# Moving transposes of a routed-attention kernel from TensorE to DMA, and re-timing its weight loads

## The chip, the cores and the metric

The kernel runs on one core of one Trainium2 chip. A core has five engines that run side by side and wait for each other through semaphores: TensorE (PE: matmuls; PEld is its weight load), VectorE (DVE), ScalarE (ACT), GpSimd (POOL) and SyncE (SP), which here only issues DMAs. The metric is the device time of one execution in microseconds (us). A profile shows one execution; its span is about 1.8 us shorter than that execution's time, because it starts with the first instruction and ends with the last. The granted clock is the share of TensorE's full clock that the execution had. A run counts as slow when it is over 1.5% above the fastest of the same kernel, and otherwise as fast; unless said otherwise all runs compared are fast ones.

## The reference

```python
# q, k, v: (4, 8, 768, 64)   centroids: (8, 16, 64)   w_in: (512, 2048)   w_out: (2048, 512)
q_assign = argmax(q_n @ c_n.T)            # each query and key gets one of 16 clusters
k_assign = argmax(k_n @ c_n.T)
scores = where(q_assign[:, None] == k_assign[None, :], q @ k.T / sqrt(64), -1e9)
attn = softmax(scores) @ v                # per batch and head: 32 "heads" in the kernel
x = attn, heads side by side              # (3072, 512)
out = gelu(x @ w_in) @ w_out              # erf form of gelu
```

## The kernel before

The kernel goes through 32 heads (4 batches of 8). Each head has six slots, one for each 128 keys. A slot does two score matmuls on PE into one of two PSUM buffers (`ps_sc`), and ACT takes their exponential. In the same slots PE does the attention-value matmuls (AV) of the head before. After the 8 heads of a batch come 16 groups of the up projection (`fc1`); the down projection (`fc2`) is spread over the slots of the next heads.

Before its slots, a head has to be prepared: POOL splits q and k into two fp16 halves (`split`), they are transposed (`T`), PE multiplies them with the centroids (`asn`), DVE makes one-hot assignments (`onehot`), and these are transposed too and put as 16 more rows into `T`, so that the score matmul adds the mask. For heads up to 11 PE does both transposes and DVE copies them out of PSUM; from head 12 on DMA transposes on the SP queue do it. The attention output of a pair of heads is transposed as well (`fin`), by PE and a DVE copy for pairs 0 to 6, by DMA from pair 8 on, but for the last pair. ("Pair 4" is heads 4 and 5.)

```python
t_pool = ctx.enter_context(tc.tile_pool(name="tT", bufs=9))
ps_sc = ctx.enter_context(tc.tile_pool(name="ps_sc", bufs=2, space=PSUM))   # scores, fc1
ps_a = ctx.enter_context(tc.tile_pool(name="ps_a", bufs=1, space=PSUM))     # assignments: one buffer
ps_o = ctx.enter_context(tc.tile_pool(name="ps_o", bufs=2, space=PSUM))     # transposes, fc2
# ... cut ...
w_chunks = [(w_in_sb[:, m], w_in_r[:, m]) for m in range(NM)]                # 8 chunks, 512 KB each
w_chunks += [(w_out_sb[:, 4 * f:4 * f + 4], w_out_r[:, 4 * f:4 * f + 4])
             for f in range(4)]
# ... cut ...
    def tr_pe(i, w, copy=None, pool=None):
        if i not in Ts:
            Ts[i] = t_pool.tile([128, 2, S], FP16, tag="T", name="T")
        st = sts[i]
        pl, tag = pool or (ps_o, "op")
        t_ps = pl.tile([128, S], FP16, tag=tag, name="tr_ps")
        for j in range(N):
            nc.tensor.transpose(t_ps[:, j * 128:(j + 1) * 128], st[:, w, j, :], ident)
        (copy or nc.vector.tensor_copy)(Ts[i][:, w, :], t_ps)
    # ... cut ...
    def tr(i):
        st = sts.pop(i)
        Ts[i] = t_pool.tile([128, 2, S], FP16, tag="T", name="T")
        nc.sync.dma_start_transpose(
            out=Ts[i].rearrange("c w (n p) -> c (w n) p", p=128),
            in_=st.rearrange("p w n c -> p (w n c)"))
    # ... cut: asn(i, which): 6 matmuls of T with the centroids, into ps_a;
    #     onehot(i): DVE adds the halves (asum), takes the maximum, compares ...
    def ohtr(i):
        oh = ohs[(i // 2) % NOH]
        ohTs[i] = t_pool.tile([128, N, 128], FP16, tag="ohT", name="ohT")
        nc.sync.dma_start_transpose(out=ohTs[i],
                                    in_=oh.rearrange("p n a b c -> p (n a b c)"))
        ohTs[i] = ohTs[i].rearrange("c n p -> c (n p)")

    def one_pe(i):
        oh = ohs[(i // 2) % NOH]
        e = i % 2
        t_ps = ps_o.tile([128, S], FP16, tag="op", name="oh_ps")
        for j in range(N):
            nc.tensor.transpose(t_ps[0:64, j * 128:(j + 1) * 128],
                                oh[:, j, e].rearrange("p b c -> p (b c)"), ident)
        nc.vector.tensor_scalar(Ts[i][D:D + C, 1, :], t_ps[32:32 + C, :],
                                -1.0, None, op0=ALU.add)
        nc.vector.tensor_scalar(Ts[i][D:D + C, 0, :], t_ps[0:C, :],
                                float(VAL), None, op0=ALU.mult)
    # ... cut: aug(i): four DVE copies from the DMA-transposed one-hots into T ...

    def scores(i, c):
        if c == 0:
            ps[i] = p_pool.tile([128, N, S], FP16, tag="p", name="p_sb")
        s_ps = ps_sc.tile([128, 2, 512], FP32, tag="sc", name="sc_ps")
        for t in range(2):
            nc.tensor.matmul(s_ps[:, t, 0:QB], Ts[i][0:D + C, 1, c * 128:(c + 1) * 128],
                             Ts[i][0:D + C, 0, t * QB:(t + 1) * QB],
                             start=True, stop=True)
        nc.scalar.activation(ps[i][:, c, :].rearrange("p (t q) -> p t q", t=2),
                             s_ps[:, :, 0:QB], ACT_FN.Exp, bias=0.0,
                             scale=float(scale))
    # ... cut ...
    def fin(i, pe=False):
        b, h = divmod(i, H)
        m = h // 2
        if m == 0:
            xts[b] = x_pool.tile([128, NM, S], FP16, tag="xt", name="xt")
        xt, x_tok = xts[b][:, m, :], xtoks.pop(i)
        if pe:
            t_ps = ps_o.tile([128, S], FP16, tag="op", name="fin_ps")
            for j in range(N):
                nc.tensor.transpose(t_ps[:, j * 128:(j + 1) * 128],
                                    x_tok[:, j].rearrange("p a d -> p (a d)"), ident)
            nc.vector.tensor_copy(xt, t_ps)
        else:
            nc.sync.dma_start_transpose(
                out=xt.rearrange("c (n p) -> c n p", p=128),
                in_=x_tok.rearrange("p n a d -> p (n a d)"))
    # ... cut ...
    def slot(i, c):
        if i < NH:
            scores(i, c)
        if i in WARM:
            warm(WARM[i])
        fill(FILL.get((i, c), 2))
        if i >= 1:
            for j in (AVS0 if i < 10 else AVS).get(c, ()):
                av(i - 1, j)
            if c == 5:
                norm(i - 1)

    def load_w(n):
        nc.gpsimd.dma_start(out=w_chunks[n][0], in_=w_chunks[n][1])
    # ... cut: every call is an event with a nominal time; they are emitted in that order,
    #     and each engine runs its own instructions in the order of emission ...
    PT = 12
    FC1 = {(9, 3): 0, (18, 0): 1, (26, 0): 2}
    # ... cut ...
            if (i, c) in FC1:
                b = FC1[i, c]
                at(t, fill, 1000)
                for f in range(NF):
                    at(t + f * 1.3, fc1, b, f)
                    if b == 0 and f % 4 == 0:
                        at(t + f * 1.3, load_w, 4 + f // 4)
                t += NF * 1.3
                at(t - 0.01, start_fc2, b)
            TS[i, c] = t
            if c == 0:
                T.append(t)
            at(t, slot, i, c)
    # ... cut ...
    for m in range(NM):
        at(T[m + 2] + 1.0, load_w, m)
    sp_t = -3.7
    for h in range(4, NH):
        pair = h - h % 2
        want = T[h - 2] - 9.0 if h < PT else T[pair] - 33.0 + 4.0 * (h % 2)
        sp_t = max(sp_t + 4.2, want)
        at(sp_t, split, h, vnow=False)
        at(sp_t + 0.02, vcast, h - 3)
        at(sp_t + 0.03, load, h + 2)
        if h >= PT:
            at(max(T[pair] - 25.0 + 2.5 * (h % 2), sp_t + 3.5), tr, h)
    for h in range(NH - 3, NH):
        at(sp_t + 0.04, vcast, h)
    for h in range(1, NH):
        pair = h - h % 2
        if h == 1:
            at(g(0, 0), tr_pe, 1, 0)
            at(g(0, 0), tr_pe, 1, 1)
            at(g(0, 2), prep_asn, h)
            at(g(0, 4), one_pe, h)
        elif h < PT:
            o = 2 if h == 2 else 0
            at(g(h - 2, 0 + o), tr_pe, h, 0)
            at(g(h - 2, 2 + o // 2), tr_pe, h, 1)
            at(g(h - 2, 4 + o // 2), prep_asn, h)
            at(g(h - 1, 1 + o // 2) if h < 11 else g(10, 4), one_pe, h)
        else:
            t0 = T[pair] - 16.5 + 2.5 * (h % 2)
            at(t0, asn, h, 0)
            at(t0 + 1.2, asn, h, 1)
            at(t0 + 1.21, onehot, h)
            if h % 2 == 1:
                at(T[pair] - 12.0, ohtr, pair)
                at(T[pair] - 5.0, aug, pair)
    for h in range(0, NH - 2, 2):
        if h < 8:
            at(g(h + 3, 3) if h < 6 else g(9, 2), fin, h, pe=True)
        else:
            at(T[h + 3] + 0.1, fin, h)
```

The softmax here doesn't subtract the row's maximum and nothing guards it: scores larger than these inputs give would overflow.

## Time and profile before

| | before |
|---|---|
| time, median of 4 fast runs (lowest to highest) | 312.58 us (312.53 to 312.83) |
| span of the profile, granted clock | 310.7 us, 1.00 |
| PE busy | 302.0 us, 97% |
| first up projection starts | 58.86 us |
| heads 2 to 8, two heads together | 9.73 us |

From the page of before: part 1 (busy time, share of the span, number of instructions), the engines of the chain that ended last (part 4), and two of the DMA issues (part 6; the last figure is the median time to landing).

```profile
PE 302.0 (97%) x3118; PEld 189.1 (61%) x3118; DVE 124.3 (40%) x289; ACT 214.7 (69%) x269; POOL 107.2 (34%) x184
...
PE 92%; DVE 5%; DMA 1%; issue 1%; ACT 0%; DVEq 0%
...
T<-st SPq DMA_TRANSPOSE x20, 4.1
xt<-x_tok SPq DMA_TRANSPOSE x11, 3.8
```

PE looks like the only limit. But shares are averages. In heads 3 to 9 the view in order of time shows ACT nearly full too (start, duration, engine, line, operation, output and input, count; idle time before it and what ended it):

```profile
30.21 9.41 ACT L297 ACTIVATE p_sb<-sc_ps 128x768 f16<-128x768 f32 x12 [0.32 <-PE sc_ps L294]
39.94 9.41 ACT L297 ACTIVATE p_sb<-sc_ps 128x768 f16<-128x768 f32 x12 [0.32 <-PE sc_ps L294]
49.66 8.56 ACT L297 ACTIVATE p_sb<-sc_ps 128x768 f16<-128x768 f32 x11 [0.31 <-PE sc_ps L294]
58.24 1.28 ACT L354 ACT_TABLE_LOAD   x1
```

Twelve exponentials are two heads. The only gap that this view shows is one of 0.32 us every two heads, in the slot in which PE does the output transposes. The same view of PE in before, at the places where the change works:

```profile
58.52 0.51 PE L332 MATMUL fin_ps<-ident,x_tok 128*128 128x128 f16 x6 [0.61 <-DVE T L260]
58.86 20.96 PE L349 MATMUL hp<-xt,w_in_sb 128*128 128x384 f16 x128
...
85.55 0.30 PE L210 MATMUL asn_ps<-c_all,T 128*128 128x32 f16 x6 [0.59 <-DVE rec L319]
...
90.30 0.52 PE L256 MATMUL oh_ps<-ident,oh_162 128*64 128x128 f16 x6
```

PE waits 0.61 us for DVE before the output transposes that stand just ahead of the first up projection (line 349), and 0.59 us behind crowded assignments after it, where it also still transposes the one-hots of head 11. The queue of SP in before shows what a head transpose can cost when weight chunks are in flight beside it (three chunks were issued between 48.9 and 54.6 us):

```profile
49.46 13.88 SPq L192 DMA_TRANSPOSE T<-st  x2
```

### The profile page before, as it was taken

Reading aid. Unit: us, or ns where it says so; the run is one execution under the profiler, and the core shown is the slowest. Engines: PE = TensorE matmul, PEld = TensorE weight load, DVE = VectorE, ACT = ScalarE, POOL = GpSimd, SP = SyncE. Lnnn points to the kernel's source line nnn. Section 1 sums busy time; section 2 is a strip of 40 time slices with the busy share of each in tenths; the row PEclk is TensorE's granted clock in tenths of the full one; section 3 lists DMA queues with packets and bytes.
Section 4 is the critical chain, followed back from the end, with each engine's and each line's share of the span. In section 5 each row is a group of like instructions: output and inputs, shape, how many; then the busy total and the mean of one; then the engine's idle time right before and its main releaser. Section 6 shows DMA issues by size and latency. Waiting matters only on the chain.

```text
span 310.7 us, 7419 instructions
## 1 busy us (share of the span) xinstructions
PE 302.0 (97%) x3118; PEld 189.1 (61%) x3118; DVE 124.3 (40%) x289; ACT 214.7 (69%) x269; POOL 107.2 (34%) x184
## 2 busy tenths in 40 slices
PE   7999999999999999999999999999999999999995
PEld 3567777666566666656566666656566655565444
DVE  5688989500356552213155552213155413100111
ACT  3689999866768888865688788865688884466000
POOL 4999999805205204444525203454000000000000
PEclk9999999999999999999999999999999999999999
DMA  7849999998049924986668824965175302000121
GB/s 221 292 154 228 213 300 217 82 161 213 2 88 250 174 54 115 190 227 95 186 131 229 169 64 134 218 207 99 29 140 71 97 34 61 36 0 2 42 94 68
DMA packets 68449, 41.87 MB, mean 135 GB/s; under 512 B 50368, under 2 KB 64960, under 8 KB 68416
## 3 DMA queue, kind: packets, MB, share of 16 engines
q1 hardware_dynamic: 65440, 37.04, 50.4%
q0 software_dynamic: 2688, 4.19, 9.3%
q8 instruction: 24, 0.39, 0.6%
q10 hardware_dynamic: 288, 0.16, 0.2%
q14 instruction: 9, 0.07, 0.1%
HBM read 27.30 MB, written 6.29 MB: 108 GB/s over the span
## 4 chain that ended last, share of the span: by engine, by line
PE 92%; DVE 5%; DMA 1%; issue 1%; ACT 0%; DVEq 0%
PE hp L349 25%; PE op L371 24%; PE sc_ps L294 20%; PE x_ps L309 12%; PE asn_ps L210 3%; PE op_alt L371 3%; PE tr_ps L149 2%; PE oh_ps L256 1%; DVE asum L223 1%; DVE asn_ps L230 1%; DMA q_raw<-in_q_dram 1%; PE fin_ps L332 1%; PE w_ps L96 1%; DVE x_tok L320 0%; DVE T L260 0%
## 5 line engine op out<-in xcount | busy, mean ns | idle before, releaser
L297 ACT ACTIVATE p_sb<-sc_ps 128x768 f16<-128x768 f32 x192 | 150.3, 809 | 25.6 <-PE sc_ps L294 16.5
L294 PE MATMUL sc_ps<-T 80*128 80x384 f16 x384 | 93.8, 325 | 0.9 <-DVE T L280 0.4
L349 PE MATMUL hp<-xt,w_in_sb 128*128 128x384 f16 x512 | 85.7, 326 | 0.0
L309 PEld LDWEIGHTS <-p_sb 128*128 128x128 f16 x1152 | 56.4, 97 | 31.7 <-issue 0.6
L349 PEld LDWEIGHTS <-w_in_sb 128*128 128x128 f16 x512 | 48.9, 97 | 31.4
L127 POOL CAST st<-q_raw 128x384 f16<-128x384 f32 x31 | 15.8, 508 | 95.4 <-DMA q_raw<-in_q_dram 95.4
L223 DVE TENSOR_REDUCE asum<-asn_ps 128x192 f32<-128x384 f32 x31 | 17.3, 558 | 65.2 <-PE asn_ps L210 65.2
L375 DVE COPY o_sb<-op 128x512 f32<-128x512 f32 (+1 forms) x22 | 14.9, 678 | 55.9 <-PE op L371 55.8
L294 PEld LDWEIGHTS <-T 80*128 80x128 f16 x384 | 26.1, 97 | 5.9 <-ACT T L284 0.5
L128 POOL TENSOR_TENSOR st<-q_raw,st 128x384 f16<-128x384 f32 x31 | 28.3, 912 | 2.5
L130 POOL TENSOR_TENSOR st<-k_raw,st 128x384 f16<-128x384 f32 x31 | 28.3, 912 | 2.5
L319 DVE RECIPROCAL rec<-x_ps 128x6 f32<-128x6 f32 x32 | 6.2, 193 | 36.1 <-PE x_ps L309 36.0
L210 PEld LDWEIGHTS <-T 128*128 128x128 f16 x372 | 14.8, 96 | 6.8 <-issue 3.0
L210 PE MATMUL asn_ps<-c_all,T 128*128 128x32 f16 x372 | 17.3, 177 | 1.5 <-DVE rec L319 0.6
L320 DVE TENSOR_TENSOR x_tok<-x_ps,rec 128x384 f16<-128x384 f32 x32 | 17.8, 558 | 1.1
L129 POOL CAST st<-k_raw 128x384 f16<-128x384 f32 x31 | 15.5, 501 | 1.0 <-DMA k_raw<-in_k_dram 1.0
L150 DVE COPY T<-tr_ps 128x768 f16<-128x768 f16 x23 | 12.5, 552 | 1.4 <-PE tr_ps L149 1.1
L149 PE MATMUL tr_ps<-ident,st 128*128 128x128 f16 x144 | 12.1, 223 | 0.1
L230 DVE TENSOR_REDUCE asn_ps<-asum 128x12 f32<-128x192 f32 x31 | 11.2, 361 | 1.1
L149 PEld LDWEIGHTS <-st 128*128 128x128 f16 x144 | 9.4, 99 | 3.1 <-DVE st L158 1.0
L266 DVE TENSOR_SCALAR T<-ohT 16x768 f16<-16x768 f16 x20 | 7.0, 351 | 6.2 <-DMA ohT<-oh_161 2.9
L96 PE MATMUL w_ps<-wz 128*128 128x512 f16 x20 | 7.7, 470 | 1.5 <-DVE wz L78 1.5
(297 smaller groups left out, 397.6 us busy)
## 6 DMA issues: line engine op xcount, KB each, us to landing
q_raw<-in_q_dram SPq DMA_DIRECT2D x32, 192.0 KB, 3.9
k_raw<-in_k_dram SPq DMA_DIRECT2D x32, 192.0 KB, 4.0
v_raw<-in_v_dram SPq DMA_DIRECT2D x32, 192.0 KB, 4.0
out_dram<-o_sb SPq DMA_DIRECT2D x23, 256.0 KB, 2.3
w_in_sb<-in_moe_w_in_dram POOLq DMA_DIRECT2D x4, 512.0 KB, 7.4
w_out_sb<-in_moe_w_out_dram POOLq DMA_DIRECT2D x4, 512.0 KB, 11.9
T<-st SPq DMA_TRANSPOSE x20, 4.1
xt<-x_tok SPq DMA_TRANSPOSE x11, 3.8
```

The source lines that it names most:

```text
L127: nc.gpsimd.tensor_copy(st[:, 0, :, 0:D], q_raw)
L128: nc.gpsimd.tensor_sub(st[:, 0, :, D:2 * D], q_raw, st[:, 0, :, 0:D])
L130: keng.tensor_sub(st[:, 1, :, D:2 * D], k_raw, st[:, 1, :, 0:D])
L149: nc.tensor.transpose(t_ps[:, j * 128:(j + 1) * 128], st[:, w, j, :], ident)
L210: nc.tensor.matmul(a_ps[:, j, which], t[:, js], c_all[:, :, chs], start=True, stop=True)
L223: nc.vector.tensor_reduce(out=asum, in_=a_ps.rearrange("p n w l c -> p n w c l"), axis=AX.X, op=ALU.add)
L294: nc.tensor.matmul(s_ps[:, t, 0:QB], Ts[i][0:D + C, 1, c * 128:(c + 1) * 128], Ts[i][0:D + C, 0, t * QB:(t + 1) * QB], start=True, stop=True)
L297: nc.scalar.activation(ps[i][:, c, :].rearrange("p (t q) -> p t q", t=2), s_ps[:, :, 0:QB], ACT_FN.Exp, bias=0.0, scale=float(scale))
L309: nc.tensor.matmul(x_ps[:, j], ps[i][:, ch, j * 128:(j + 1) * 128], va[:, ch, :], start=(ch == 0), stop=(ch == N - 1))
L320: nc.vector.tensor_tensor(xtoks[i - i % 2][:, :, i % 2, :], x_ps[:, :, 0:D], rec.to_broadcast([128, N, D]), op=ALU.mult)
L349: nc.tensor.matmul(hp[:, t, 0:QB], w_in_sb[:, m, f * 128:(f + 1) * 128], xts[b][:, m, t * QB:(t + 1) * QB], start=(m == 0), stop=(m == NM ...
L371: nc.tensor.matmul(op[:, 0:w], gs[b][f][:, js], w_out_sb[:, f, ms], start=(f == 0), stop=(f == NF - 1))
```

## The change

Its intent: take transposes from PE where PE and DVE are full (heads 10 and 11, output pairs 0 to 2, that is `fin` of heads 0, 2 and 4) and give them to DMA; and load the weight chunks at other times, so that the DMA is free for the new transposes. Two of the chunks are held back: DVE writes one column of the chunk's destination first, so the load has to wait for DVE to come to that point.

```diff
--- before.py
+++ after.py
@@ -423,11 +423,15 @@
     def load_w(n):
         nc.gpsimd.dma_start(out=w_chunks[n][0], in_=w_chunks[n][1])
 
+    def hold_w(n):
+        nc.vector.memset(w_out_sb[:, 4 * (n - NM), 0:1], 0.0)
+
     def start_fc2(b):
         filler[0] = fc2(b)
 
 
-    PT = 12
+    PT = 10
+    WOUT_F = (2, 8, )
     FC1 = {(9, 3): 0, (18, 0): 1, (26, 0): 2}
     events = []
 
@@ -443,8 +447,10 @@
                 at(t, fill, 1000)
                 for f in range(NF):
                     at(t + f * 1.3, fc1, b, f)
-                    if b == 0 and f % 4 == 0:
-                        at(t + f * 1.3, load_w, 4 + f // 4)
+                    if b == 0 and f in WOUT_F:
+                        n = NM + 4 - len(WOUT_F) + WOUT_F.index(f)
+                        at(t + f * 1.3, hold_w, n)
+                        at(t + f * 1.3 + 0.01, load_w, n)
                 t += NF * 1.3
                 at(t - 0.01, start_fc2, b)
             TS[i, c] = t
@@ -470,7 +476,9 @@
         onehot(h)
 
     for m in range(NM):
-        at(T[m + 2] + 1.0, load_w, m)
+        at(T[m] + 6.0, load_w, m)
+    for n, w_t in enumerate((T[6] + 1.0, T[8] + 1.0, )):
+        at(w_t, load_w, NM + n)
     sp_t = -3.7
     for h in range(4, NH):
         pair = h - h % 2
@@ -497,16 +505,21 @@
             at(g(h - 2, 4 + o // 2), prep_asn, h)
             at(g(h - 1, 1 + o // 2) if h < 11 else g(10, 4), one_pe, h)
         else:
-            t0 = T[pair] - 16.5 + 2.5 * (h % 2)
-            at(t0, asn, h, 0)
-            at(t0 + 1.2, asn, h, 1)
-            at(t0 + 1.21, onehot, h)
+            if pair < 10:
+                at(g(pair - 2, 3) if h % 2 else g(pair - 3, 5), prep_asn, h)
+                to, tg = T[pair] - g(pair - 2, 5), T[pair] - g(pair - 1, 2)
+            else:
+                ta, to, tg = (16.5, 12.0, 5.0) if pair >= 12 else (12.5, 7.0, 3.0)
+                t0 = T[pair] - ta + 2.5 * (h % 2)
+                at(t0, asn, h, 0)
+                at(t0 + 1.2, asn, h, 1)
+                at(t0 + 1.21, onehot, h)
             if h % 2 == 1:
-                at(T[pair] - 12.0, ohtr, pair)
-                at(T[pair] - 5.0, aug, pair)
+                at(T[pair] - to, ohtr, pair)
+                at(T[pair] - tg, aug, pair)
     for h in range(0, NH - 2, 2):
-        if h < 8:
-            at(g(h + 3, 3) if h < 6 else g(9, 2), fin, h, pe=True)
+        if h == 6:
+            at(g(9, 2), fin, h, pe=True)
         else:
             at(T[h + 3] + 0.1, fin, h)
```

In this kernel `pair < 10` never holds where the new branch for it stands, so that branch does nothing.

## The prediction

> **What bounds it.** TensorE (PE). The page's busy table gives PE 302.0 of 310.7 us; the stage table shows PE full in nearly every stretch from 22 us on, clock 1.00. The Trainium skill (Perfetto Trace Analysis, "Identifying the Most-Contended Engine") warns that matmul occupancy overstates this; PEld is only 61%. But the chain of waits is 92% PE and PE's timeline has almost no gaps, so PE work removed counts, unless another engine is as full. In heads 2 to 9 one is: ACT runs 12 exponentials in 9.41 us, against a period of two heads of 9.73 us.
>
> **What changes.**
> - Output pairs 0, 2, 4 lose their PE transposes (about 0.41 us of PE timeline each) and a 0.56 us DVE copy. With ACT's floor each is worth 0.32 us: 1.0 us.
> - Heads 10 and 11 lose four PE transposes (0.34 us each), two one-hot transposes (0.42 to 0.45 us) and their DVE copies. Between head 8 and the first up projection (58.86 us) PE sheds four transposes, one one-hot, one assignment (0.30 us), and the 0.61 us wait for DVE before the last output transposes: 2.7 us. ACT binds again there (11 exponentials, 8.6 us), so I expect 1.2 us, and the up projection starting near 56.7 us, 2.2 us earlier in all.
> - The assignments of heads 10 and 11 move into the up projection, where DVE is idle: +0.6 us there, -0.3 us after it.
> - After it, head 11's one-hot transposes (0.45 us) and the 0.59 us wait behind crowded assignments (around 85 us) go: -1.0 us.
> - DMA gains three output, two head and one one-hot transpose (uncontended landings 3.8, 4.1, 2.8 us, from the table of issues), all on the SP queue. Weight chunks go out earlier, the last two only after small writes that DVE makes once the last output copy is done (about 57 us). POOL waits with them, so heads 12 and 13 are split at about 57 to 64 us.
>
> After 92 us the programs are nearly the same and PE is dense, so the lead is kept.
>
> Sum: -2.2 + 0.6 - 0.3 - 1.0 = -2.9 us. I give 0.3 us back for new stalls: **309.9 us**, 8 in 10 between **308.9 and 311.4**. Faster by over 2%: 0.02; within 2%: 0.96; slower: 0.02.
>
> **Where DMA could spoil it.** Before, two head transposes issued at 49.5 us beside the weight chunks held the SP queue for 13.9 us, and one landed 19.4 us after issue. The skill (DMA: Bandwidth & Descriptors, "Queues, rings and completion order") says that each DMA engine goes round-robin between queue rows packet by packet; the trace agrees that the two slow each other. The change keeps heads 10 and 11 clear of the chunks, but heads 12 and 13 (about 61 to 66 us) meet the last two. Needed: head 12 by about 77 us, the one-hot of pair 10 by about 82, the last chunk by about 83. I expect all to arrive, with little room.
>
> **What would show it.** Matmuls 3118 to 3064. ACT without 0.3 us gaps in heads 3 to 8. Up projection at 56.4 to 57.2 us, lasting 21.4 us instead of 20.8. No wait of PE over 0.3 us at 77 to 90 us. Second up projection at 128 to 128.5 instead of 131.0; later stages unchanged in length.
>
> **What would make it wrong.** PE stalls of 1 us or more at 77 to 90 us on head 12's transpose, on DVE behind the pair's one-hot transpose, or on the last chunk. SP, blocked by output transposes, loading heads 9 to 11 so late that POOL's splits starve PE (margin now about 10 us). ACT idling after all in heads 3 to 8.

## The result

| | before | after |
|---|---|---|
| time, median of 4 fast runs | 312.58 us (312.53 to 312.83) | 309.97 us (309.64 to 310.07) |
| ratio, 95% interval | | 0.9913 (0.9896 to 0.993) |
| span of the profile, granted clock | 310.7 us, 1.00 | 307.9 us, 1.00 |
| PE instructions | 3118 | 3064 |

A ratio is the mean time of one kernel's fast runs over that of the other's fast runs of the same rounds, so it is not quite the ratio of the medians that are quoted. The result is faster by 0.9%, which is "the same" by the 2% rule, as forecast.

The same parts of the page of after:

```profile
PE 298.9 (97%) x3064; PEld 186.1 (60%) x3064; DVE 120.0 (39%) x284; ACT 214.1 (70%) x269; POOL 107.2 (35%) x184
...
PE 88%; DVE 4%; ACT 3%; DMA 2%; issue 1%; POOL 0%; DVEq 0%
...
T<-st SPq DMA_TRANSPOSE x22, 4.5
xt<-x_tok SPq DMA_TRANSPOSE x14, 3.1
```

PE lost 54 instructions and 3.1 us of busy time. ACT and DMA now appear in the chain. ACT in order of time, after:

```profile
21.44 35.29 ACT L297 ACTIVATE p_sb<-sc_ps 128x768 f16<-128x768 f32 x46 [0.16 <-PE sc_ps L294]
56.74 1.28 ACT L354 ACT_TABLE_LOAD   x1
```

The three gaps of 0.32 us are gone: 46 exponentials stand in one row. PE in order of time, after, around the first up projection and at one later place:

```profile
55.89 0.50 PE L332 MATMUL fin_ps<-ident,x_tok 128*128 128x128 f16 x6
56.22 11.94 PE L349 MATMUL hp<-xt,w_in_sb 128*128 128x384 f16 x72
67.99 0.31 PE L210 MATMUL asn_ps<-c_all,T 128*128 128x32 f16 x6
...
69.60 1.46 PE L349 MATMUL hp<-xt,w_in_sb 128*128 128x384 f16 x8
71.28 0.30 PE L210 MATMUL asn_ps<-c_all,T 128*128 128x32 f16 x6 [0.22 <-DVE oh_162 L231]
...
78.08 0.30 PE L210 MATMUL asn_ps<-c_all,T 128*128 128x32 f16 x6
...
171.91 0.32 PE L210 MATMUL asn_ps<-c_all,T 128*128 128x32 f16 x6 [0.20 <-DMA T<-st]
```

The assignments of heads 10 and 11 are now inside the up projection, one of them waits for the one-hot of the head before, and at 172 us PE waits for a head transpose by DMA, which it did not in before.

The profiles start unevenly: the first score matmuls, before anything that the change touches, came at 9.91 us in before and 10.04 us in after (and at up to 10.66 us in the profiles of the experiments). So I measure the stages from the first score matmuls:

| from the first score matmuls to | before | after | difference |
|---|---|---|---|
| start of the first up projection | 48.95 | 46.18 | -2.77 |
| its end | 69.75 | 68.04 | -1.71 |
| start of the second up projection | 120.96 | 117.49 | -3.47 |
| start of the third | 190.64 | 187.53 | -3.11 |
| start of the fourth | 255.64 | 252.53 | -3.11 |

(The end is the start of the first PE instruction after it.) So 2.77 us are gained before the first up projection, 1.06 us are given back in it, 1.76 us are gained after it, and 0.36 us are lost later. The SP queue in after, for the head transposes of pairs 10 and 12:

```profile
53.31 8.60 SPq L192 DMA_TRANSPOSE T<-st  x2
...
65.10 8.00 SPq L192 DMA_TRANSPOSE T<-st  x2
```

They are slowed by the chunks and the loads, as feared (against 3.2 us for two in a quiet stage later), but none held PE up here: the longest landing of a head transpose was 9.0 us, against 19.4 us in before.

### The profile page after: what moved, and what is told of

It reads as the page before. It is cut to its first block, busy times and chain, and to the rows that moved or that the text cites. A ratio compares the mean times of both kernels' runs of the same rounds, so it can differ in the third digit from the quotient of the medians.

```text
span 307.9 us, 7323 instructions
## 1 busy us (share of the span) xinstructions
PE 298.9 (97%) x3064; PEld 186.1 (60%) x3064; DVE 120.0 (39%) x284; ACT 214.1 (70%) x269; POOL 107.2 (35%) x184
## 4 chain that ended last, share of the span: by engine, by line
PE 88%; DVE 4%; ACT 3%; DMA 2%; issue 1%; POOL 0%; DVEq 0%
PE hp L349 25%; PE op L371 23%; PE sc_ps L294 19%; PE x_ps L309 11%; PE asn_ps L210 3%; PE op_alt L371 3%; ACT p_sb L297 3%; PE tr_ps L149 2%; DMA T<-st 2%; PE oh_ps L256 1%; DVE asum L223 1%; DMA q_raw<-in_q_dram 1%; DVE asn_ps L230 1%; DVE oh_160 L231 0%; PE w_ps L96 0%
## 5 line engine op out<-in xcount | busy, mean ns | idle before, releaser
L309 PEld LDWEIGHTS <-p_sb 128*128 128x128 f16 x1152 | 56.4, 97 | 31.6 <-issue 0.6
L266 DVE TENSOR_SCALAR T<-ohT 16x768 f16<-16x768 f16 x22 | 7.7, 352 | 9.3 <-DMA ohT<-oh_161 3.1
L150 DVE COPY T<-tr_ps 128x768 f16<-128x768 f16 x19 | 10.3, 552 | 1.3 <-PE tr_ps L149 1.1
L149 PE MATMUL tr_ps<-ident,st 128*128 128x128 f16 x120 | 10.1, 223 | 0.3 <-DVE st L158 0.3
L149 PEld LDWEIGHTS <-st 128*128 128x128 f16 x120 | 7.9, 99 | 2.9 <-DVE st L158 1.2
```

Of the source, the lines that this page charges most:

```text
L309: nc.tensor.matmul(x_ps[:, j], ps[i][:, ch, j * 128:(j + 1) * 128], va[:, ch, :], start=(ch == 0), stop=(ch == N - 1))
```

## The experiments

Twelve kernels ran. "Ratio" is always to the kernel before, run in the same rounds on the same chip.

### Parts of the change alone

**weights_only**: only the weight chunks, without any transpose moved.

```diff
 (to before)
-        at(T[m + 2] + 1.0, load_w, m)
+        at(T[m] + 6.0, load_w, m)
+    for n, w_t in enumerate((T[6] + 1.0, T[8] + 1.0, )):
+        at(w_t, load_w, NM + n)
 ... and hold_w with the two chunks at f in (2, 8), as in the change
```

> Only the weight chunks' new times and the two small writes, everything else as before. Theory A (the gain is TensorE work taken away down to ScalarE's floor, plus two waits for VectorE; the chunks' times only keep the DMA clear): 312.6 us, ratio 0.999 to 1.001. Rival B (the gain comes from the weights no longer colliding with the head transposes): ratio 0.992 to 0.996.

Measured: 312.57 us, ratio 0.9998 (0.9986 to 1.001). The weights alone gain nothing. Rival B, that the gain comes from a freer DMA, is out.

**fins_only**: only output pairs 0, 2 and 4 by DMA.

```diff
 (to before)
-        if h < 8:
-            at(g(h + 3, 3) if h < 6 else g(9, 2), fin, h, pe=True)
+        if h == 6:
+            at(g(9, 2), fin, h, pe=True)
```

> Only output pairs 0, 2 and 4 by DMA transposes. Theory A: ScalarE's exponentials become continuous in heads 3 to 8 and bind, so each pair is worth its 0.32 us gap: -1.0 us, ratio 0.9968 (0.996 to 0.9975). Rival C (TensorE alone binds): 0.41 us each plus nothing else lost, -1.25 us, ratio 0.996. If the output transposes hold up the loads: ratio over 0.998.

Measured: 311.51 us, ratio 0.996 (0.9948 to 0.9973). In its trace the first up projection starts 47.71 us after the first scores, 1.24 us earlier than in before. That is what rival C said (1.25 us), more than my floor allowed (1.0 us).

**heads_only**: only heads 10 and 11 by DMA (`PT = 10` and their new times), output pairs and chunks as before.

```diff
 (to before)
-    PT = 12
+    PT = 10
 ... and the branch with ta, to, tg of the change
```

> Only heads 10 and 11 by DMA transposes; output pairs by TensorE and weight chunks as before. Theory A: up projection about 1.7 us earlier, 1.0 us longer, and 1.7 us less after it: -2.4 us, less about 0.3 us that the trace of after lost to a late transpose of a later pair: ratio 0.992 to 0.9945. Theory A also says that if the chunks are needed where they now are, head 10 or 11's transpose lands after TensorE asks for it (about 68 and 71 us) and TensorE waits over 1 us in the first up projection: then ratio over 0.996. Rival B: no gain, ratio 0.999 to 1.001.

Measured: 311.02 us, ratio 0.9946 (0.9934 to 0.9958), just outside the range that I gave. The first up projection starts 1.55 us earlier; a wait of 0.43 us for a head transpose at 162 us takes part of the later gain back. There was no collision in the first up projection: without the output transposes, the SP queue got to the transposes of heads 10 and 11 at 42.1 us, before the four chunks of `w_out` (44.9 to 54.0 us). The two halves add up: 1.24 + 1.55 = 2.79 us, against 2.77 us in after.

**no_weights**: the whole change, but the weight chunks go out as before.

```diff
 (to after)
-        at(T[m] + 6.0, load_w, m)
-    for n, w_t in enumerate((T[6] + 1.0, T[8] + 1.0, )):
-        at(w_t, load_w, NM + n)
+        at(T[m + 2] + 1.0, load_w, m)
 ... and the load_w of before at f % 4 == 0, without hold_w
```

> The whole change but for the weight chunks, which go out as before. Theory A without a collision: as after, ratio 0.990 to 0.993. Theory A with a collision: a head transpose takes over 10 us to land, TensorE waits 1 us or more in the first up projection or just after it, ratio 0.994 to 0.999. Rival B: ratio over 0.998.

Measured: 312.33 us, from 310.95 to 316.28 us in six runs (the 316.28 us run counts as slow), ratio 0.9989 (0.9953 to 1.0025): no gain that is clear of the noise. Its profile is of a run of 315.11 us at clock 0.992. Its SP queue and PE in order of time:

```profile
50.71 14.66 SPq L192 DMA_TRANSPOSE T<-st  x2
```

```profile
74.98 0.32 PE L210 MATMUL asn_ps<-c_all,T 128*128 128x32 f16 x6 [3.98 <-DMA T<-st]
```

The collision is real in this execution; the other four fast runs (310.95 to 312.46 us) have no trace, so how large it was in them is not known. The output transposes hold up the SP queue, so the transposes of heads 10 and 11 are issued at 50.7 us; chunks go out at 48.8, 53.8 and twice at 58 us; one transpose lands 22.4 us after issue, and PE stands still for 3.98 us. So the new times of the chunks gain nothing by themselves, but the two other parts together need them. The Trainium skill (DMA: Bandwidth & Descriptors, "Issuing engines are not separate DMA queues") says that DMAs from different engines share the same 16 DMA engines and interleave. This trace agrees: POOL's chunks took an SP transpose from a usual 4.4 us (this profile's median) to 22.4 us.

**no_hold**: after, without the two small writes.

```diff
 (to after)
-                        at(t + f * 1.3, hold_w, n)
```

> The kernel after without the two small writes, so that the last two chunks go out as soon as GpSimd comes to them (about 54 us instead of 57 and 65). Theory A: if the writes are needed, the transposes of heads 10 and 11 (issued at 53 us) land later than 9 us after issue and TensorE waits at about 68 to 72 us, 0.5 to 3 us lost. If they are not, the same as after within 0.3 us.

Measured: 309.76 us, ratio 0.9905 (0.989 to 0.992); after's own, in other rounds, was 0.9913. The third chunk of `w_out` went out at 47.3 instead of 57.3 us; the longest landing of a head transpose grew to 11.8 us, and PE still did not wait for it. The hold gave nothing that these runs can show. What counts is the earlier order of the chunks.

### What binds in heads 3 to 8

**before_less_av** and **after_less_av** leave out 12 of the 36 AV matmuls of heads 3 to 6. Their outputs are wrong, which doesn't matter for the times.

```diff
 (to before, and to after)
-        for ch in range(N):
+        n = N - 2 if 3 <= i <= 6 else N
+        for ch in range(n):
             nc.tensor.matmul(x_ps[:, j], ps[i][:, ch, j * 128:(j + 1) * 128],
-                             va[:, ch, :], start=(ch == 0), stop=(ch == N - 1))
+                             va[:, ch, :], start=(ch == 0), stop=(ch == n - 1))
```

> Wrong result on purpose: the kernel before with 12 of 36 attention-value matmuls left out for heads 3 to 6, which takes 0.39 us of TensorE time from each of the four slots (1.6 us). Theory A (ScalarE's exponentials are the floor in these heads): only the two slots that also hold an output transpose gain, 0.32 us each: -0.6 us. Rival C (TensorE alone binds): -1.6 us.

> Wrong result on purpose: the kernel after with the same 12 of 36 matmuls left out for heads 3 to 6. Theory A: ScalarE is already continuous there, so nothing is gained: 309.7 to 310.1 us, within 0.2 us of after. Rival C: -1.6 us, about 308.4 us.

Measured: before_less_av 313.29 us, ratio 1.002 (1.0003 to 1.0036). after_less_av 310.74 us, ratio 0.9935 (0.992 to 0.995), above the 309.7 to 310.1 us that I expected. Neither gained; both are even a little slower. The traces tell where: in before_less_av the last output transposes before the up projection come 48.45 us after the first scores instead of 48.61 us, so 0.16 us of the 1.6 us cut is gained; the start (10.45 us) and a wait of 0.27 us for a head transpose at 176 us cost more than that. In after_less_av the 46 exponentials take 35.25 us instead of 35.29 us, so nothing is gained, and two later waits for head transposes (0.35 and 0.40 us) remain. So in the heads without output transposes TensorE's work is not what binds alone: there rival C is out. My theory A said "no gain" for after_less_av, but -0.6 us for before_less_av, which was wrong too.

For the slots with output transposes before_less_av is a weak test. The 12 matmuls are spread over a head's slots, and such a slot lost only 4 of its 12 (0.13 us, if 12 take 0.39 us), so it could not have gained 0.32 us. The views in order of time of DVE and PE show where even that got stuck; first before, then before_less_av:

```profile
38.46 0.55 DVE L260 TENSOR_SCALAR T<-oh_ps 16x768 f16<-16x768 f16 x1
39.07 0.51 PE L332 MATMUL fin_ps<-ident,x_tok 128*128 128x128 f16 x6
39.62 0.56 DVE L334 COPY xt<-fin_ps 128x768 f16<-128x768 f16 x1
40.43 0.56 DVE L223 TENSOR_REDUCE asum<-asn_ps 128x192 f32<-128x384 f32 x1 [0.25 <-PE asn_ps L210]
```

```profile
38.98 0.55 DVE L260 TENSOR_SCALAR T<-oh_ps 16x768 f16<-16x768 f16 x1
39.59 0.51 PE L333 MATMUL fin_ps<-ident,x_tok 128*128 128x128 f16 x6
```

In both, PE starts the output transposes 0.06 us after DVE has finished the second copy of one-hots (line 260): that copy frees one of the two PSUM buffers of `ps_o`. (At pair 6, at 58.52 us in before, the wait is long enough for the view to name this copy.) From there the way leads through PE (output transposes, scores, AV, assignments) back to DVE (line 223). So in before the transposes lie on this way, while DVE's own copy of their result (line 334) is done 0.25 us before DVE can go on.

The starts of single exponentials show why after_less_av gained nothing. The view in order of time joins instructions with short gaps between them; taken from the trace one by one, the intervals of the exponentials' starts in us are, over two heads in the steady part and at the end of the stage:

```
before          1.13 .82 .77 .71 .79 .86   .71 .82 .77 .71 .79 .86    two heads: 9.74
fins_only        .71 .82 .77 .71 .79 .86   .71 .82 .77 .71 .79 .86               9.32
after            .71 .82 .77 .71 .79 .86   .71 .82 .77 .71 .79 .86               9.32
after_less_av    .71 .86 .71 .69 .87 .82   .71 .86 .71 .69 .87 .82               9.32
after, last six before the table load:  .69 .69 .77 .71 .69
```

ACT can go at 0.69 to 0.71 us an exponential. The 9.41 us for twelve that I took for ACT's floor holds small gaps; ACT was not the floor in heads 3 to 8. With fewer AV matmuls the intervals change places, but their sum, 4.66 us a head, stays. Something else has that period. DVE in order of time, in after_less_av, over one head:

```profile
34.28 0.56 DVE L150 COPY T<-tr_ps 128x768 f16<-128x768 f16 x1
35.25 0.56 DVE L223 TENSOR_REDUCE asum<-asn_ps 128x192 f32<-128x384 f32 x1 [0.41 <-PE asn_ps L210]
35.84 0.36 DVE L230 TENSOR_REDUCE asn_ps<-asum 128x12 f32<-128x192 f32 x1
...
38.35 0.55 DVE L260 TENSOR_SCALAR T<-oh_ps 16x768 f16<-16x768 f16 x1
38.93 0.56 DVE L150 COPY T<-tr_ps 128x768 f16<-128x768 f16 x1
39.90 0.56 DVE L223 TENSOR_REDUCE asum<-asn_ps 128x192 f32<-128x384 f32 x1 [0.41 <-PE asn_ps L210]
```

It is a loop: DVE copies the second transpose of a head (line 150), PE can then do the assignments of that head, DVE waits 0.41 us for them, and then does the nine instructions that end with the next such copy. From 35.25 to 39.90 us it takes 4.65 us. PE in order of time shows the other half of it; first after_less_av, then after:

```profile
39.18 0.68 PE L210 MATMUL asn_ps<-c_all,T 128*128 128x32 f16 x12
```

```profile
39.24 0.45 PE L210 MATMUL asn_ps<-c_all,T 128*128 128x32 f16 x12
```

With PE relieved, the twelve assignment matmuls take 0.68 instead of 0.45 us: PE comes early and waits inside the group for DVE's copy. In after it comes just as the copy ends, and has no gap. So in a head without output transposes two limits of nearly the same length stand side by side: the loop through DVE (4.65 us), and the slots of PE (4.66 us).

**fins_dummy_pe** tests theory D at the output pairs. The output pairs go by DMA as in fins_only, so DVE's copies are gone, but PE still does the 18 transposes.

```diff
 (to fins_only)
+    def fin_again(i):
+        t_ps = ps_o.tile([128, S], FP16, tag="op", name="again_ps")
+        for j in range(N):
+            nc.tensor.transpose(t_ps[:, j * 128:(j + 1) * 128],
+                                kept[i][:, j].rearrange("p a d -> p (a d)"), ident)
+        if h < 6:
+            at(g(h + 3, 3), fin_again, h)
```

> As fins_only (output pairs 0, 2, 4 by DMA), but TensorE still does the 18 transposes in their old places, into a PSUM tile that nobody copies: only VectorE's three copies are taken away. Theory D (formed after the runs with fewer attention-value matmuls: in heads 3 to 8 the period of a head is a loop of nine VectorE instructions, 4.24 us, plus 0.42 us in which VectorE waits for the assignment matmuls, 4.66 us in all; TensorE and ScalarE have slack beside it): nearly all of fins_only's gain stays, ratio 0.995 to 0.9968. Theory C (TensorE's transposes are what the pair cost): ratio 0.999 to 1.001.

Measured: 312.96 us in its fast runs, ratio 1.0006 (0.9993 to 1.002). The profiled run fell into a slow state of its own (513.23 us at clock 0.56), so no trace of it is used. No gain at all, as theory C said: theory D as I had stated it, that DVE's loop binds and PE has slack, is wrong as well. fins_dummy_pe differs from fins_only only by the 18 transposes on PE, and they take back the whole gain (ratio 1.0006 against 0.996; for want of a fast trace the place is not seen). So these transposes are what the output pairs cost, and DVE's copies off alone gain nothing. Whether the copies would matter once the transposes are gone was not tested: no run takes away the transposes and keeps the copies. The 0.25 us that DVE has to spare in before allow an estimate: of the 0.42 us that a pair cost, the transposes alone would give about 0.25 us, and the rest needs the copies gone too. Why PE's side is so tight is what the next run shows.

**after_oh_late** moves the one-hot transposes of heads 3 to 9 two slots later. No work is added or taken away.

```diff
 (to after)
-            at(g(h - 1, 1 + o // 2) if h < 11 else g(10, 4), one_pe, h)
+            at(g(h - 1, 3) if h > 2 else g(1, 2), one_pe, h)
```

> As after, but the one-hot transposes of heads 3 to 9 are put two slots later, so that VectorE's two one-hot copies (1.13 us) run while TensorE does the assignments, instead of VectorE waiting 0.42 us. No work is added or taken away on any engine. Theory D: the head's period falls from 4.66 us towards 4.3 us, where ScalarE's 0.70 us an exponential or TensorE's own work stops it: first up projection 0.7 to 2.5 us earlier, ratio to before 0.983 to 0.989. Theory C (TensorE's work binds): as after, 0.990 to 0.9925.

Measured: 313.33 us, ratio 1.0021 (1.0007 to 1.0034), some 3.4 us slower than after, which neither theory had expected. PE in order of time, over the two slots that matter:

```profile
34.59 0.55 PE L309 MATMUL x_ps<-vaug,p_sb 128*128 128x65 f16 x12
35.08 0.52 PE L256 MATMUL oh_ps<-ident,oh 128*64 128x128 f16 x6
35.53 0.50 PE L294 MATMUL sc_ps<-T 80*128 80x384 f16 x2
...
37.75 0.48 PE L294 MATMUL sc_ps<-T 80*128 80x384 f16 x2
38.52 0.48 PE L294 MATMUL sc_ps<-T 80*128 80x384 f16 x2 [0.29 <-ACT p_sb L297]
```

The transposes now share a slot with twelve AV matmuls; in this kernel the exponentials' intervals are .82 .77 .71 .69 .91 1.27, in sum 5.17 us. The slot that lost them has nothing between two pairs of score matmuls, and there PE waits for ACT to free a score buffer. With two score buffers and PE in order, a light slot cannot lend its time to a heavy one. So PE's limit is not its total work (which is the same here and in after) but what stands in each slot: near 0.70 us ACT sets the pace of a slot, above it PE does.

### The waits that were left

**after_spaced** puts one more up-projection group between the assignments of the two heads of a pair.

```diff
 (to after)
-                ta, to, tg = (16.5, 12.0, 5.0) if pair >= 12 else (12.5, 7.0, 3.0)
-                t0 = T[pair] - ta + 2.5 * (h % 2)
+                ta, to, tg = (17.9, 12.0, 5.0) if pair >= 12 else (13.9, 7.0, 3.0)
+                t0 = T[pair] - ta + 3.9 * (h % 2)
```

> The kernel after with the second head's assignments 3.9 instead of 2.5 units behind the first's (one more up-projection group between them), starting 1.4 units earlier. Theory A's remainder: in the up projections TensorE waits 0.22 us (0.38 us of its timeline) for the one-hot of the head before, five times; the spacing should take all five away: -1.5 to -1.9 us against after, about 308.3 us, ratio to before 0.986 to 0.9875. If the waits only move: same as after.

Measured: 308.75 us, ratio 0.9872 (0.9858 to 0.9887), near the upper end of what I expected; against after (in other rounds) that is about 1.2 us, less than the 1.5 to 1.9 us expected. All five waits of 0.22 us for a one-hot are gone. But another wait grew. From the table of waits of PE (who waited for whom, total us, times, longest), after_spaced:

```profile
PE asn_ps L210 <- DMA T<-st: 1.0, 1, 1.0
PE sc_ps L294 <- ACT p_sb L297: 0.9, 4, 0.3
```

PE now asks for the transpose of a later head (at 170.6 us) 1.0 us before it has landed. The SP queue had issued it at 165.84 us, right behind a one-hot transpose that waits for DVE, although POOL had the data ready about 15 us earlier (at 150.65 us).

**spaced_early** also puts the head transposes 3 units earlier in the queue.

```diff
 (to after_spaced)
-            at(max(T[pair] - 25.0 + 2.5 * (h % 2), sp_t + 3.5), tr, h)
+            at(max(T[pair] - 28.0 + 2.5 * (h % 2), sp_t + 3.5), tr, h)
```

> As after_spaced, with the head transposes put 3 units earlier in the SP queue, ahead of the one-hot transpose of the pair before. If the 1.0 us that TensorE waited for a head transpose at 171 us in after_spaced is a matter of when the SP queue gets to it, that wait goes: 0.8 to 1.2 us faster than after_spaced, ratio to before 0.982 to 0.985. If it is DMA throughput, or the earlier transposes collide with the weight chunks: 0.986 or more.

Measured: 308.23 us, ratio 0.9857 (0.9844 to 0.9871), correct, the fastest of all. That is a little less gain than I expected. The table of waits of its PE has no wait for a DMA any more:

```profile
PE w_ps L96 <- DVE wz L78: 1.5, 1, 1.5
PE sc_ps L294 <- ACT p_sb L297: 0.9, 4, 0.3
```

In the traces the stage from the second to the third up projection takes 68.92 us, against 70.08 us in after_spaced and 70.04 us in after. So the wait was a matter of order in the queue, not of DMA throughput. Of those 1.16 us, about 0.5 us show in the time; this profile's first scores came 0.65 us later than after_spaced's. Whether that is chance or belongs to the kernel stays open.

**all_three** adds the later one-hot transposes to spaced_early.

> The kernel after with the spaced assignments, the earlier head transposes and the later one-hot transposes together. If the three are independent, their gains add: about 306 us under theory D, ratio 0.975 to 0.983; under theory C as spaced_early.

Measured: 311.37 us, ratio 0.9965 (0.9952 to 0.9977): about 3.1 us slower than spaced_early, and outside what either theory said. The loss of after_oh_late carries over nearly whole; the gains of the other two edits stand beside it.

## Why the prediction was right or wrong

The time was right: 309.9 us forecast, 309.97 us measured, inside 308.9 to 311.4 us. The parts were less right, and their errors partly cancelled, so that the forecast came within 0.1 us is luck in part.

| term of the sum | forecast | traces |
|---|---|---|
| before the first up projection | -2.2 | -2.77 |
| - from the output pairs | -1.0 | -1.24 (fins_only) |
| - from heads 10 and 11 | -1.2 | -1.55 (heads_only) |
| inside the first up projection | +0.6 | +1.06 |
| after it | -1.3 | -1.76 |
| new stalls | +0.3 | +0.36 |
| sum | -2.6 | -3.11 |

The sum of the traces is to the start of the third and fourth up projections; the measured times differ by 2.6 us. The later start of after's profile (0.13 us) and an end of the program that comes 0.13 us later relative to the last copy make 2.85 us of the 3.11 us in the spans.

- **The reason for the output pairs was wrong, and their size too small.** The step that failed is "with ACT's floor each is worth 0.32 us". ACT's pace is 0.69 to 0.71 us, not 9.41 / 12 = 0.78 us. What each pair cost was one interval of 1.13 instead of 0.71 us: 0.42 us. fins_dummy_pe and fins_only show that PE's transposes cost it. That DVE's copies had to go too for the full 0.42 us is an estimate from the trace of before, not shown by a run.
- **Heads 10 and 11** were mis-sized by the same step. At the end of the stage, where PE and DVE have both lost work, ACT does bind, and PE waits for it three times (0.18, 0.21 and 0.27 us), but at its true pace. The up projection began at 56.22 us, just earlier than my 56.4 to 57.2 us.
- **The first up projection.** The four groups of assignments cost 0.16 us each, 0.63 us, as forecast. The term that I left out is a wait for the one-hot of the first head: 0.22 us in the profile, 0.38 us of PE's timeline, since the end of a matmul covers the start of a gap. The other up projections of before already showed that wait, so it could have been foreseen. after_spaced shows that spacing takes it away.
- **After it**, the gain was larger: the assignments 0.31 us, the wait 0.75 us of timeline where the profile says 0.59 us, the one-hot transposes 0.55 us with a small gap before them, and 0.15 us in the slot behind. PE had no wait over 0.3 us at 77 to 90 us, as forecast. The second up projection began at 127.5 us, just earlier than forecast.
- **DMA.** The transposes of pair 12 met the last chunks at 65 us and all arrived in time, as forecast. That the change "keeps heads 10 and 11 clear of the chunks" was wrong: their transposes landed 8.9 and 9.0 us after issue (the median in this profile is 4.5 us), and a chunk went out at 57.3 us between issue and landing; but they came in time. That this took the chunks' new times is shown by the one trace of no_weights (3.98 us of wait). That the two held writes are needed is not shown; no_hold speaks against it.
- **Later stages** were not unchanged: an earlier PE asked for a later head's transpose 0.2 us (0.36 us of timeline) before it landed. The stall that I had priced at 0.3 us came, but not where I had looked for it.

On the rule of the Trainium skill (Perfetto Trace Analysis, "Identifying the Most-Contended Engine") to optimize the engine with the highest occupancy first, and for TensorE to look at MFU (useful work against peak) and weight-load time instead: in heads 3 to 8 a cut of AV on PE gained at most 0.16 of 1.6 us. At 32 to 37 us in before PE was busy all 5 us and its weight loads 3.62 us; neither tells of the second limit, a loop through DVE, whose own busy share there was about 0.9 (4.37 of 5 us). The section's remark that matmul busy time is not a good measure of how close PE is to its roofline (the best that the hardware allows) agrees with after_less_av, where PE lost a third of AV in four heads and still showed 4.94 of 5 us busy in the same stretch. The skill's hint on interleaving regimes (the same page, "Optimization Strategy") fits what worked: the assignments of two heads moved into the up projection, where DVE did nothing for 22.5 us in before.

## What to carry to other kernels

A stretch without visible gaps is not proof that its engine is the floor: look at single starts, and compare with the fastest pace that the same instruction reaches anywhere in the trace. When two limits of nearly equal length run side by side, taking work from one alone can gain nothing, as in after_less_av. What a cut is worth depends on where it lies: 1.6 us of AV off PE gained 0.16 us, while 18 transposes that stood between two steps of DVE's loop were worth 1.24 us. Giving a transpose to DMA also saves the copy out of PSUM; that this copy would have been the next limit is likely from the trace, but was not tested. When a stage becomes faster, check the DMA queue's order for the next consumers: a transfer whose data are ready can sit behind one that waits.

## What the Trainium skill lacked or had wrong

- Perfetto Trace Analysis, "Identifying the Most-Contended Engine": it gives no test for two limits that bind at once. Here a loop through DVE (4.65 us a head) was as long as PE's slots (4.66 us), and a cut of 1.6 us of AV on PE shortened the stretch of exponentials by 0.04 us (after_less_av).
- The same page, "Optimization Strategy", looks for gaps between slices. Gaps below about 0.16 us are covered by the pipelined ends of matmuls here: a wait listed as 0.22 us cost 0.38 us of timeline, one listed as 0.59 us cost 0.75 us.
- DMA: Bandwidth & Descriptors, "DMA Transpose (X-bar)": it has no figure for a DMA transpose beside plain DMAs of another queue. Here a head transpose landed in 4.1 us (median of before), and in up to 22.4 us beside weight chunks issued from GpSimd (no_weights); its issue alone held the SP queue for up to 14.66 us for two.
- TensorE: Matmul & The Clock Gate, "Seeing it yourself", tells of a clock seen stuck at a quarter for 50 us and more. Here one whole execution was slow: 513.23 us at mean granted clock 0.56, where the other runs of the same kernel took 312.56 to 312.96 us. Its cause was not looked into.
